# A fused cross-covariance attention and GELU feed-forward kernel: 137 sevenfold sets for 125, one sum of the second product held in PSUM, squares and scalings moved between two engines, and a new order

## The chip, the core and the metric

The kernel runs on one core of one Trainium2 chip. A core has TensorE (PE in the profile; its weight loads are shown apart as PEld), VectorE (DVE), ScalarE (ACT), GpSimd (POOL) and SyncE (SP). Each takes its instructions strictly in the order in which the program gives them, and waits where one of them needs something that is not there yet. SP, POOL and ACT also issue DMA transfers. The metric is the device time of one execution in microseconds (us). Before the change it is 689.86 us, the median of three runs from 689.82 to 689.93.

## What is computed

The reference, cut to what matters:

```python
B, N, C = 4, 6080, 256                   # q, k, v: (B, N, C); w_in: (256, 2048); w_out: (2048, 256)
qn = q / (norm(q, axis=1) + 1e-6)        # norms over the 6080 tokens
kn = k / (norm(k, axis=1) + 1e-6)
s = kn.transpose(0, 2, 1) @ qn / tau     # 256 x 256 for each batch
a = softmax(s)
x = (v @ a).reshape(24320, 256)
h = x @ w_in                             # 24320 x 2048
out = gelu_tanh(h) @ w_out               # 24320 x 256
```

## The kernel before

**Folding.** The kernel never forms x. For each of the four batches it computes `AW = a @ w_in` (256 x 2048, bf16), so that the first product is `v @ AW` and the second `gelu(v @ AW) @ w_out`. The tokens are cut into 25 blocks (`SB`): 23 of 1024 or 960 tokens and two last ones of 512 and 448. A block is two halves of `hc` tokens (512, 480, 256 or 224), and each half is the free side of a matmul.

**First product of a block.** The 2048 features are 16 chunks `fc` of 128, in eight pairs `p`. A pair takes one of two ways. The direct way, `mm1_one` (step `j`, L550 to L558), is two matmuls for one chunk and one half, followed by one Gelu on ACT (`gelu_one`, step `J`, L561 to L570); a pair has four of these, eight matmuls in all. The other way is a *set* (`small` L601, `set_step` L624): seven matmuls `m1` to `m7` on sums of the weights (`sums_w`, DVE) and of the tokens (`sums_v`, DVE) give the same four results, a Strassen-like scheme. In return a set has two more copies on ACT (`cq`, L636, from the sum `rb` into a second PSUM bank `qa`; `y5`, L639, from the bank `qb` into SBUF) and two additions on DVE (`ap`, L641; `ax`, L644). It ends with four Gelus (`G0` L646, `G1` L649, `Gr` L652, `Gx` L655), as the direct way does. Where `cq` puts a copy under a running sum, matmuls on zeros first mark those parts of the bank that no matmul wrote at full width before (L630 to L635).

**Second product of a block.** It is the same scheme at a larger size: DVE forms sums of Gelu results (`sums_g`, steps `T1` to `T4`, each in halves a and b), then come seven products `M1` to `M7` of eight matmuls each, in halves A and B (`product`, L720). They go to three PSUM sums: `u` takes M1, M6, M7 and M4, `p` takes M5 and M3, `c` takes M2 alone (`BANK`, L718). After M1, `x1` copies `u` into SBUF on ACT (`keep`, L737 to L742). After M2, `a11` adds that copy to `c` on DVE (`add_out`, L744 to L748) and `c11` transposes the sum into the output tile (`turn`, L750). `ap`, `ax`, `c12`, `c21` and `c22` do the like for the other quarters. `O0` and `O1` store the rows.

**The next batch's weights.** While a batch is worked on, q and k of the next are loaded (`lq`, `lk`, from POOL's queue), multiplied (`r`: one gram row is two matmuls of 256 columns, L292), squared on ACT (`zq`, `zk`, `square_later`, L253 to L264) and folded on DVE (`f`, L272 to L284). A chain of small steps then gives the exponentials `eT`; `aw` multiplies them with w_in (L498), and `ac` scales the result out of PSUM, for batches 1 to 3 on ACT where the part is in `AW_ACT` (L509) and else on DVE (L511). `lv` casts v through DRAM (POOL's queue, L305), and `lt` loads it transposed (SP's queue, L317).

**The start.** Batch 0 has a path of its own: gram and squares as its rows arrive, then the loads of v, w_in (`win_bf`) and w_out (`wst`, two of 1 MB) on POOL's queue, `scores`, and `first_aw` (L364 to L394), which gives the first 512 of the 2048 columns of `AW`; then the Gelu table is loaded on ACT (L876).

**Order and banks.** After that, the whole program is one list written out by hand, `ORDER`, of 3958 steps such as `12:s5m3` (block 12, set 5, matmul m3), `b2:zq4` or `7:M1A`. Each engine gets its instructions in the order of that list. The eight PSUM banks (`a` to `h`) are handed out in the order in which they were given back (`take`, `give`), so a step that takes a bank waits for the last reader of the bank that came free longest ago.

Of the kernel before, what the change touches and what calls it, by code (L numbers as in the profile page):

```python
# [18 lines left out]
def kernel(  # L19
# [10 lines left out]
    nc = tc.nc  # L30
# [222 lines left out]
    def square_later(b, c, which):  # L253
        n = chunk(c)[1]
        if (b, c) not in SQ:
            SQ[b, c] = sqp.tile([128, CH, 512], BF16, tag="sq", name=f"sq{b}_{c}")
            if n < CH:
                nc.vector.memset(SQ[b, c][REM:, n, :], 0.0)
        t = qk_tiles[b, c, which]
        parts = [(128, slice(0, n))]  # L260
        if n < CH:
            parts.append((REM, slice(n, n + 1)))
        for np_, r in parts:
            nc.scalar.activation(SQ[b, c][:np_, r, which * 256 : which * 256 + 256], t[:np_, r, :], AF.Square)  # L264
# [99 lines left out]
    def first_aw():  # L364
# [21 lines left out]
        for f in range(2):  # L386
            for ic in range(2):
                o = AW[b][:, ic, f * 256 : f * 256 + 256]
                if (f, ic) == (0, 1):
                    nc.scalar.activation(o, ps[f][ic], AF.Copy, scale=rs[:, ic : ic + 1])  # L390
                else:
                    nc.vector.tensor_scalar_mul(o, ps[f][ic], rs[:, ic : ic + 1])
# [178 lines left out]


# [51 lines left out]
    def set_step(m, p, what):  # L624
# [3 lines left out]
        if what == "cq":  # L628
            Q0[m, p], tag = take(("q0", m, p), 1, [128, 512], f"qa{m}_{p}", width=None)
            while WIDTH.get(tag, 0) < hc:  # L630
                w = WIDTH.get(tag, 0)
                e = min(hc, w + 256)
                nc.tensor.matmul(Q0[m, p][:, w:e], lhsT=ones_bf, rhs=zeros_bf[:, 0 : e - w],
                                 start=w == 0, stop=True, skip_group_check=True)
                WIDTH[tag] = e  # L635
# [84 lines left out]
    def product(m, i, half):  # L720
        hc = SB[m][2]
        acc = BANK[i]
        first = (m, acc) not in STARTED
# [11 lines left out]
    XS, CS, OT = {}, {}, {}  # L735

# [33 lines left out]
    def mm2_step(m, what):  # L770
# [3 lines left out]
        elif what == "x1":  # L774
            keep(m, "u", "x1")
# [8 lines left out]
        elif what == "a11":  # L784
            add_out(m, "c", "x1", 0, 0)
            give(("c", m))
# [3 lines left out]
        else:  # L790
            ci, tj = {"c22": (1, 1), "c11": (0, 0), "c12": (0, 1), "c21": (1, 0)}[what]
            if (m, ci, tj) in CS:
                turn(m, ci, tj, CS.pop((m, ci, tj)))
            else:
                acc = {"c12": "p", "c21": "u"}[what]
                turn(m, ci, tj, ACCS[m, acc])
                give((acc, m))

    with tc.manual_schedule():
# [64 lines left out]
        for f0, f1 in ((0, 256), (256, 512), (512, 1024), (1024, 1536), (1536, 2048)):  # L864
            nc.gpsimd.dma_start(out=win_bf[:, :, f0:f1], in_=wi[:, :, f0:f1])
        load_wout(0)
        load_v0(0, 1)
# [6 lines left out]
        pe_vt_copy(0, 0, 1)  # L874
        first_aw()
        nc.scalar.preload_act_table(AF.Gelu_apprx_tanh)  # L876
# [7 lines left out]
        def step(b, what):  # L884
# [9 lines left out]
            elif what[:2] in ("zq", "zk"):  # L894
                square_later(b, int(what[2:]), "qk".index(what[1]))
# [66 lines left out]
1:j31 1:J41 0:J41 0:s7Gx 1:vs1 1:j20 b1:r0.1 1:J21 0:M5A b1:r0.2 1:J31 b1:zq0 b1:r0.3 b0:w03 b1:zk0
0:T2a b1:lk3 1:s3m5 0:M1B b1:r1.0 0:T3b b1:r1.1 1:J20 0:x1 2:lt0 0:T1b b1:lq3 b1:r1.2 1:j11 :pS2
0:T2b 0:M5B b1:zq1 0:M6A 0:y5 1:s3cq 3:lt1 0:M6B 0:ap 1:J11 b1:f0.1 1:s3m6 b1:r1.3 0:T4a b1:lq4
1:s3y5 1:vs2 1:J51 1:s3ap 1:s3m2 1:s4m5 1:s3G0 b1:zk1 0:M7A 1:s4m1 0:M3A 1:s4y5 0:M7B 1:s4cq b1:r2.0
b1:f1.1 b1:zq2 3:lt0 1:s3m7 1:s4m6 0:ax 1:s4m2 b1:r2.1 1:s4ap 1:s3ax b1:zk2 1:s4G0 b1:r2.2 0:T4b
1:s3m3 b1:lk4 0:M3B 1:s4m3 1:s5m1 1:s4m7 b1:f1.2 b1:zk3 0:M4A 1:s4G1 1:s3G1 1:s3Gx 0:c12 1:s3m4
1:s5cq 1:s5m5 1:s4ax 0:M4B 1:s3Gr b1:f2.1 1:s5m2 1:s4Gx b1:r2.3 1:s5y5 b1:lk5 1:s5m6 1:s4m4 0:c21
1:s5G0 b1:r3.0 1:s5ap 1:s4Gr 1:s6m1 1:s6m5 0:M2A 1:s5m7 b1:lq6 b1:zq3 b1:f1.3 1:s6y5 1:s5ax 1:s5m3
b1:r3.1 b1:r3.2 0:M2B b1:r3.3 0:c22 1:s6cq 4:lv1 1:s5G1 1:s6m6 1:s7m1 1:s5Gx 1:s7cq 0:a11 1:s5m4  # L970
1:s6m2 1:s6ap 1:T3a 1:s5Gr b1:lq5 b1:r4.0 b1:r4.1 1:s7m5 1:s6m7 1:s7m6 1:s6G0 1:s6m3 1:s7m2 1:s7y5
1:s6ax 4:lv0 1:s7ap b1:r4.2 2:j20 1:s6G1 2:j51 2:s3m1 1:s6m4 b1:r4.3 1:s7m3 1:s7G0 1:s6Gx 1:s7m7
1:M1A 2:J20 2:j00 1:s7G1 b1:f3.1 b1:f3.2 b1:f3.3 1:s6Gr 2:s3cq 1:s7ax 2:J51 1:T1a 2:j10 1:s7m4
1:s7Gx 1:M1B 2:J00 2:vs0 2:s3m2 1:s7Gr 2:j41 2:s3G0 2:j01 2:j11 2:J10 1:T3b 2:j30 2:J01 1:M5A 2:s3m5
2:J30 b1:r5.0 1:T1b 2:j31 2:vs1 2:J11 2:J41 2:j40 2:vs2 2:s3m6 2:s3y5 1:x1 1:T2a 2:J31 2:s3ap 2:s4m1
b1:lk6 1:T2b 1:M5B 2:J40 1:y5 2:s3m7 1:M6A 2:s3m3 2:s4m5 1:M6B b1:r5.1 2:s3ax 2:s4cq 2:s3m4 b1:zk4
2:s4m6 2:s3G1 2:s4y5 2:j21 2:s4m2 1:T4a 2:s3Gx 2:s3Gr 1:ap 2:J21 1:M7A 2:s4ap 2:s4m7 1:T4b 2:s5m5
b1:lk7 2:s4m3 2:s5m1 1:M3A b1:zk5 1:M3B 2:s4G1 1:M7B b1:r5.2 2:s5y5 b1:zq5 2:s5cq b1:zq4 b1:f3.4
2:s4ax 2:s4m4 2:s5m2 0:c11 1:c12 b1:r5.3 6:lv0 2:s4G0 b1:lk8 0:O1 2:s5m6 1:ax 1:M4A 2:s5ap 2:s5G0
4:lt1 2:s6m1 b1:lq7 b1:f5.1 2:s4Gx 2:s5m3 2:s6cq 2:s6m5 2:s5G1 1:c22 2:s5m7 2:s6y5 1:M4B 2:s4Gr  # L980
2:s5ax b1:lq8 2:s5Gx 1:c21 2:s6m2 2:j50 2:s5m4 2:s6G0 2:T3a b1:zq6 2:s6m6 b1:r6.0 2:s7m5 2:s6ap
1:M2A 2:s7m1 2:s5Gr 2:J50 1:M2B 2:s6m3 2:s6m7 2:s7cq b1:f4.1 1:O1 b1:r6.1 3:j50 1:a11 b1:r6.2 3:j10
2:s7y5 2:s6G1 3:J50 2:s6ax 2:s7m6 1:c11 3:j31 b1:r6.3 0:O0 3:J10 2:s7m2 2:s6Gx 2:s7ap 2:T1a 2:M1A
2:s7m7 2:s7G0 2:s6m4 2:s7m3 3:j01 2:s7ax b1:zk6 b1:r7.0 3:J31 b1:zk7 b1:r7.1 b1:r7.2 2:s7Gx b1:r7.3
2:T2a 2:M1B 3:j21 2:s7G1 2:s6Gr 2:s7m4 b1:f5.2 3:j30 3:J01 2:s7Gr 3:j51 b1:f6.1 2:T3b 3:J21 3:j00
3:j20 2:x1 3:J00 2:M5A 3:s3m1 3:J51 3:J20 2:T1b 3:vs0 2:T2b 3:s3cq b1:lq9 3:vs1 2:M5B b1:f5.3 3:j40
3:s3m5 3:J30 2:y5 3:s3y5 2:M6A 3:J40 3:s3m2 3:s3G0 3:s4m1 3:s4cq b1:zq7 2:T4a 3:s3m6 b1:r8.0 2:M6B
3:s3ap 3:vs2 b1:lq10 2:ap 3:s3m3 3:s4m5 3:s4y5 3:s3m7 3:s4m6 3:s3ax 3:s4m2 b1:lk9 1:O0 3:s4G0 3:s3Gx
3:s4ap 2:M7A 2:M3A b1:zk8 3:s4m7 3:s3m4 3:s3G1 3:s3Gr 3:j11 2:M7B 3:s4ax 3:J11 3:j41 3:s4Gx 3:s5m5
2:T4b b1:r8.1 2:M3B b1:f5.4 3:s4m4 b1:lk10 2:ax 3:s5m1 3:J41 b1:zq8 b1:f7.1 3:s4m3 2:c12 2:M4A  # L990
3:s5cq b1:r8.2 3:s4Gr 3:s5m2 3:s5m6 b1:f7.2 2:c22 3:s5y5 3:s5ap 3:s6m1 2:M4B 3:s4G1 3:s5G0 3:s6m5
b1:f7.3 3:s6cq 3:s5m7 b1:f7.4 b1:zq9 2:M2A 3:s6y5 3:s6m6 b1:r8.3 b1:r9.0 3:s6m2 2:M2B 2:c21 b1:zk9
4:lt0 3:s5ax 3:s5m3 6:lv1 3:s6ap 3:s6G0 3:s6m7 3:s7m1 3:s5Gx b1:f8.1 4:j10 2:a11 3:s5G1 3:s6m3
b1:lk11 3:s5m4 3:s7cq b1:r9.1 3:s7m5 b1:r9.2 4:J10 b1:r9.3 3:s6ax 3:s7y5 3:s6G1 b1:lq11 3:s6m4
3:s7m2 3:s7m6 b1:r10.0 4:j11 3:T3a 3:s6Gx 3:s6Gr b1:f9.1 3:s7ap 4:J11 3:M1A 3:s7m7 3:s5Gr 3:T1a
3:s7m3 4:j00 3:M1B 4:s3m1 3:s7G1 4:j50 3:s7ax 3:T2a 3:s7m4 4:J00 b1:f9.2 4:j40 3:s7Gx 3:x1 b1:r10.1
3:T3b 7:lv1 4:vs0 4:J50 4:s3cq 4:J40 3:T1b 3:M6A 3:s7Gr 4:j30 3:s7G0 4:vs1 4:s3m2 4:j41 4:s3m5
# [280 lines left out]
```

## Time and profile before

| | before |
|---|---|
| median of 3 runs | 689.86 us |
| the profiled execution | 689.49 us, of which the span from first to last instruction is 687.7 us |
| granted TensorE clock | 0.998 of full speed |
| TensorE busy | 667.5 us in 3483 matmuls |
| VectorE busy | 623.9 us in 916 instructions |
| ScalarE busy | 632.8 us in 1205 instructions |
| first direct matmul of block 0 | 37.58 us after the start of the span |
| first matmul of the second product | 62.88 us |
| 16 DMA engines | 78.80 MB, 115 GB/s mean |

An instruction's duration in the profile is not its price where an engine has the next one ready: a matmul of 512 columns is recorded with 0.379 us and the next begins 0.216 us after it; Gelus of 512 columns, recorded with 0.66 to 0.69 us, follow each other every 0.49 us. The prices below are such distances from start to start. The rows of the engines therefore add up to more than the engine's busy time.

### The profile page before, as it was taken

The numbers are of one execution on the slowest core, as the hardware profiler recorded it, in microseconds if no ns is written. First come the engines' busy times: TensorE is split into PE (matmuls) and PEld (weight loads), VectorE is DVE, ScalarE is ACT, GpSimd is POOL, SyncE is SP. The second block draws the span as 40 slices with busy tenths as digits, with TensorE's granted clock in tenths as the row PEclk, the third lists the DMA queues.
The fourth block names the chain that finished last, engine by engine and source line by source line (L and its number), as shares of the span: only waits on it lengthen the run. The fifth ranks groups of instructions, "written<-read, shape, count | busy, mean of one in ns | idle before, by whom it ended". The sixth has DMA issues, their size and how long they took to land.

```text
span 687.7 us, 10235 instructions
## 1 busy us (share of the span) xinstructions
PE 667.5 (97%) x3483; PEld 334.9 (49%) x3483; DVE 623.9 (91%) x916; ACT 632.8 (92%) x1205; POOL 89.1 (13%) x163
## 2 busy tenths in 40 slices
PE   3989999999999999999999999999999999999997
PEld 2844445454445455444444545445444444444455
DVE  3589898999998899999999998999999999999995
ACT  5389999999999999999989999999989999999963
POOL 4331211121000212020001102111000000000001
PEclk9999999999999999999999999999999999999999
DMA  9999677649564899854454789850828524433416
GB/s 241 208 264 167 100 120 132 113 81 157 94 99 86 140 180 153 151 86 77 91 99 73 130 145 162 153 90 17 131 38 157 95 51 86 73 58 61 74 34 118
DMA packets 165093, 78.80 MB, mean 115 GB/s; under 512 B 148992, under 2 KB 153472, under 8 KB 164320
## 3 DMA queue, kind: packets, MB, share of 16 engines
q0 software_dynamic: 18000, 39.72, 34.8%
q1 hardware_dynamic: 145792, 37.14, 29.5%
q10 hardware_dynamic: 1248, 1.28, 0.6%
q8 instruction: 27, 0.44, 0.3%
q14 instruction: 26, 0.21, 0.1%
HBM read 78.91 MB, written 36.57 MB: 168 GB/s over the span
## 4 chain that ended last, share of the span: by engine, by line
PE 88%; DMA 7%; ACT 4%; issue 0%; DVE 0%; POOL 0%; ACTq 0%; POOLq 0%
PE u L732 23%; PE j L557 15%; PE rb L616 15%; PE p L732 11%; PE qb L616 7%; PE c L732 6%; PE G L292 4%; DMA qk<-in_k_dram 4%; PE qa L616 4%; PE awp L498 2%; DMA k<-in_k_dram 1%; ACT g L569 1%; DMA win_bf<-in_moe_w_in_dram 1%; ACT sq L264 1%; ACT g L649 0%
## 5 line engine op out<-in xcount | busy, mean ns | idle before, releaser
L732 PEld LDWEIGHTS <-wcomb 128*128 128x128 bf16 x1400 | 136.8, 98 | 142.8 <-issue 1.1
L569 ACT ACTIVATE g<-j 128x512 bf16<-128x512 f32 (+1 forms) x252 | 154.1, 672 | 4.0 <-PE j L557 3.2
L557 PE MATMUL j<-vT,aw 128*128 128x512 bf16 (+2 forms) x552 | 147.8, 376 | 1.1 <-ACT g L569 0.5
L732 PE MATMUL u<-t,wcomb 128*128 128x512 bf16 (+3 forms) x600 | 145.6, 368 | 0.0
L732 PE MATMUL p<-g,wcomb 128*128 128x512 bf16 (+3 forms) x400 | 97.2, 368 | 0.0
L641 DVE TENSOR_TENSOR qb<-rb,yw 128x512 f32<-128x512 f32 (+2 forms) x125 | 84.3, 679 | 8.4 <-ACT yw L639 3.3
L616 PE MATMUL rb<-tv,sw 128*128 128x512 bf16 (+2 forms) x250 | 91.0, 374 | 0.0
L644 DVE TENSOR_TENSOR xw<-rb,yw 128x512 f32<-128x512 f32 (+2 forms) x125 | 83.1, 669 | 6.3 <-PE rb L616 4.1
L636 ACT ACTIVATE qa<-rb 128x512 f32<-128x512 f32 (+2 forms) x125 | 80.1, 643 | 5.6 <-PE rb L616 4.1
L655 ACT ACTIVATE g<-xw 128x512 bf16<-128x512 f32 (+2 forms) x125 | 83.8, 674 | 1.1 <-DVE xw L644 1.0
L649 ACT ACTIVATE g<-qb 128x512 bf16<-128x512 f32 (+2 forms) x125 | 79.5, 642 | 5.5 <-PE qb L616 5.3
L557 PEld LDWEIGHTS <-aw 128*128 128x128 bf16 x552 | 53.8, 98 | 59.8 <-issue 3.8
L639 ACT ACTIVATE yw<-qb 128x512 f32<-128x512 f32 (+2 forms) x125 | 78.7, 638 | 2.0 <-PE qb L616 1.8
L646 ACT ACTIVATE g<-qa 128x512 bf16<-128x512 f32 (+2 forms) x125 | 79.4, 643 | 1.1 <-PE qa L616 0.9
L652 ACT ACTIVATE g<-rb 128x512 bf16<-128x512 f32 (+2 forms) x125 | 79.7, 644 | 0.2
L616 PEld LDWEIGHTS <-sw 128*128 128x128 bf16 x500 | 48.9, 98 | 52.4 <-issue 1.1
L713 DVE TENSOR_TENSOR t<-g,g 128x2048 bf16<-128x2048 bf16 (+3 forms) x50 | 57.9, 1158 | 3.5 <-ACT g L566 2.2
L305 POOL DMA_DIRECT2D vb<-in_v_dram x47 | 24.2, 515 | 270.4 <-PE rb L616 164.1
L705 DVE TENSOR_TENSOR g<-g 128x2048 bf16<-128x2048 bf16 (+3 forms) x50 | 58.1, 1163 | 0.4
L711 DVE TENSOR_TENSOR t<-g,g 128x2048 bf16<-128x2048 bf16 (+3 forms) x50 | 58.1, 1164 | 0.3
L715 DVE TENSOR_TENSOR t<-t,g 128x2048 bf16<-128x2048 bf16 (+3 forms) x50 | 57.5, 1159 | 0.1
L616 PEld LDWEIGHTS <-aw 128*128 128x128 bf16 x375 | 36.7, 98 | 37.8
(131 smaller groups left out, 1005.5 us busy)
## 6 DMA issues: line engine op xcount, KB each, us to landing
out_dram<-ot SPq DMA_DIRECT2D x160, 128.0 KB, 3.2
vb<-in_v_dram POOLq DMA_DIRECT2D x37, 256.0 KB, 4.7
k<-in_k_dram POOLq DMA_DIRECT2D x33, 256.0 KB, 4.7
q<-in_q_dram POOLq DMA_DIRECT2D x33, 256.0 KB, 5.4
out_dram<-ot SPq DMA_DIRECT2D x24, 120.0 KB, 4.8
wst<-in_moe_w_out_dram POOLq DMA_DIRECT2D x2, 1024.0 KB, 11.0
qk<-in_q_dram POOLq DMA_DIRECT2D x3, 512.0 KB, 14.5
qk<-in_k_dram POOLq DMA_DIRECT2D x3, 512.0 KB, 17.1
```

The source lines that it names most:

```text
L557: GATE[0] = nc.tensor.matmul(hp[:, :n].rearrange("p (t x) -> p t x", t=2) if t == 2 else hp[:, :n], lhsT=AW[b][:, cc, fc * 128 : fc * 128 ...
L569: nc.scalar.activation(g[:, t, fc % 8, :hc], hp[:, :hc], AF.Gelu_apprx_tanh)
L616: GATE[0] = nc.tensor.matmul(acc[:, :hc], lhsT=lhs, rhs=rhs, start=i in (1, 5), stop=True, skip_group_check=True)
L636: nc.scalar.activation(Q0[m, p][:, :hc], RB[m, p][:, :hc], AF.Copy)
L639: nc.scalar.activation(YW[m, p][:, :hc], Q1[m, p][:, :hc], AF.Copy)
L641: nc.vector.tensor_add(Q1[m, p][:, :hc], RB[m, p][:, :hc], YW[m, p][:, :hc])
L644: nc.vector.tensor_add(XW[m, p][:, :hc], RB[m, p][:, :hc], YW.pop((m, p))[:, :hc])
L646: nc.scalar.activation(g[:, 0, e, :hc], Q0.pop((m, p))[:, :hc], AF.Gelu_apprx_tanh)
L649: nc.scalar.activation(g[:, 1, e, :hc], Q1.pop((m, p))[:, :hc], AF.Gelu_apprx_tanh)
L652: nc.scalar.activation(g[:, 0, e + 1, :hc], RB.pop((m, p))[:, :hc], AF.Gelu_apprx_tanh)
L655: nc.scalar.activation(g[:, 1, e + 1, :hc], XW.pop((m, p))[:, :hc], AF.Gelu_apprx_tanh)
L732: GATE[0] = nc.tensor.matmul(ACCS[m, acc][:, :hc], lhsT=wcomb[:, w, fc, :], rhs=x[:, fc, :], start=first and k_ == 0, stop=k_ == 3, skip_g ...
```

## The change

Six parts of the text change, and the order.

- `square_later` takes a flag. `zq` and `zk` square on ACT as before; the new step `dk` squares the same piece of k with a multiplication on DVE. In the new order the even pieces of k (18 of 36) are `dk`.
- `AW_ACT` holds all eight parts: the scalings `ac` of batches 1 to 3 are all on ACT. There are 24 of these; 12 were on DVE.
- `first_aw` scales its first 256 columns on DVE in four pieces of 128 and its last 256 on ACT in two. Before it was three pieces of 256 on DVE and one on ACT.
- The Gelu table is loaded ahead of `first_aw` in place of behind it.
- The second piece of v for block 0 is loaded ahead of the first part of w_out.
- `x1` becomes `split_off`: the copy of `u` goes on ACT into a PSUM bank `c` of its own, M2 adds to it there, `a11` is gone and `c11` transposes straight from that bank. The marking of a bank becomes a helper, `flagged`.
- The list: 4017 steps. Counted by kind, what differs is this.

| steps | before | after |
|---|---|---|
| `j` and `J` (direct chunk and its Gelu; 2 matmuls, 1 ACT) | 252 each | 204 each |
| `m1` to `m7`, `cq`, `y5`, `ap`, `ax`, four Gelus (sets) | 125 each | 137 each |
| `a11` | 25 | 0 |
| `zk`, `dk` | 36, 0 | 18, 18 |

The new sets are number 2 of blocks 2 to 4 and 7 to 18 (15 sets, in blocks 11 and 17 with 480 columns). Block 0 loses set 5, and blocks 20 and 22 lose set 1 (three sets of 512 columns). All other steps are as many as before and stand in another order.

```diff
-    def square_later(b, c, which):
+    def square_later(b, c, which, on_act):
...
-            nc.scalar.activation(SQ[b, c][:np_, r, which * 256 : which * 256 + 256], t[:np_, r, :], AF.Square)
+            o = SQ[b, c][:np_, r, which * 256 : which * 256 + 256]
+            if on_act:
+                nc.scalar.activation(o, t[:np_, r, :], AF.Square)
+            else:
+                nc.vector.tensor_mul(o, t[:np_, r, :], t[:np_, r, :])
...
-        for f in range(2):
+        for u in range(2):
             for ic in range(2):
...
+                nc.vector.tensor_scalar_mul(AW[b][:, ic, u * 128 : u * 128 + 128],
+                                            ps[0][ic][:, u * 128 : u * 128 + 128], rs[:, ic : ic + 1])
+        for ic in range(2):
+            nc.scalar.activation(AW[b][:, ic, 256:512], ps[1][ic], AF.Copy, scale=rs[:, ic : ic + 1])
...
+    def flagged(t, tag, hc):
+
+        while WIDTH.get(tag, 0) < hc:
+            w = WIDTH.get(tag, 0)
+            e = min(hc, w + 256)
+            nc.tensor.matmul(t[:, w:e], lhsT=ones_bf, rhs=zeros_bf[:, 0 : e - w],
+                             start=w == 0, stop=True, skip_group_check=True)
+            WIDTH[tag] = e
...
-        first = (m, acc) not in STARTED
+        first = acc != "c" and (m, acc) not in STARTED
...
+    def split_off(m):
+
+        hc = SB[m][2]
+        ACCS[m, "c"], tag = take(("c", m), 1, [128, HALF], f"c{m}", width=None)
+        flagged(ACCS[m, "c"], tag, hc)
+        nc.scalar.activation(ACCS[m, "c"][:, :hc], ACCS[m, "u"][:, :hc], AF.Copy)
...
         elif what == "x1":
-            keep(m, "u", "x1")
+            split_off(m)
...
-        elif what == "a11":
-            add_out(m, "c", "x1", 0, 0)
-            give(("c", m))
...
-                acc = {"c12": "p", "c21": "u"}[what]
+                acc = {"c11": "c", "c12": "p", "c21": "u"}[what]
...
+        load_v0(0, 1)
         load_wout(0)
-        load_v0(0, 1)
         load_v0(1, 0)
...
+        nc.scalar.preload_act_table(AF.Gelu_apprx_tanh)
         first_aw()
-        nc.scalar.preload_act_table(AF.Gelu_apprx_tanh)
...
-AW_ACT = (1, 3, 5, 7)
+AW_ACT = (0, 1, 2, 3, 4, 5, 6, 7)
 ORDER = """
...
-0:j00 b0:aw2 2:lv1 b0:aw3 b0:aw4 b0:ac2 0:j10 b0:aw5 b0:ac4 1:lv1 0:J00 0:j30 0:s5m1 0:J10 0:J30
...
+0:j00 b0:aw3 b0:aw2 0:j30 b0:ac3 0:j10 b1:lq0 b0:ac2 b0:aw5 3:lv0 0:j20 0:J30 b1:lk0 1:lv1 0:J20
...
```

Two stretches of the lists that the prediction refers to, around `x1` of block 20. Before: `20:M1B 20:s7Gx 19:a11 20:s7m4 20:s7m3 20:T2a 21:s2cq 21:j01 21:vs0 20:s7G1 21:j00 20:T3b 21:s2m2 20:M5A 20:s7Gr 21:vs1 21:s1m5 21:J01 21:j11 20:x1 20:M6A`. After: `20:M1B 19:M4B 20:s6G1 21:vs0 20:s7G1 20:s7Gr 21:s1m1 21:s2m1 21:J00 21:J10 21:s1m5 23:lv1 20:T1a 21:vs1 20:x1 21:J01 19:c21 21:s1cq 21:s2cq 20:M2A`.

## The prediction, made before the changed kernel was run

> **What bounds the kernel now.** I read the page's shares first, then the busy time by stretches, then the chain that ended last, and last what TensorE itself waited for.
>
> ```profile
> PE 667.5 (97%) x3483; PEld 334.9 (49%) x3483; DVE 623.9 (91%) x916; ACT 632.8 (92%) x1205; POOL 89.1 (13%) x163
> ...
> PE 88%; DMA 7%; ACT 4%; issue 0%; DVE 0%; POOL 0%; ACTq 0%; POOLq 0%
> ```
>
> Three engines are over 90% busy, so shares alone decide nothing. The chain is 88% TensorE. The stretches (busy us of each engine; the last numbers are clock, DMA share and GB/s) show where it is not:
>
> ```profile
> 37.60:62.90 25.30, 22.00 (x108) 9.63 (x109) 21.94 (x37) 22.89 (x43) 6.56 (x11) 1.00 1.16 240
> 62.90:100.00 37.10, 36.98 (x190) 18.45 (x190) 34.13 (x47) 37.10 (x68) 5.29 (x10) 1.00 0.73 116
> 100.00:650.00 550.00, 550.00 (x2712) 264.43 (x2711) 520.96 (x750) 535.02 (x1026) 58.21 (x107) 1.00 0.62 104
> ```
>
> From 100 to 650 us TensorE has no gap while ScalarE is busy 97% and VectorE 95%: a removed matmul is worth its full distance there, and the two others have 15 and 29 us to spare. Distances from start to start, in the chain and on ScalarE's time line:
>
> ```profile
> 80.14 0.86 PE u L732 x4
> ...
> 103.60 1.73 PE p L732 x8
> ```
>
> ```profile
> 219.94 0.58 ACT L639 ACTIVATE yw<-qb 128x512 f32<-128x512 f32 x1
> 220.42 0.60 ACT L649 ACTIVATE g<-qb 128x512 bf16<-128x512 f32 x1
> 220.89 0.64 ACT L655 ACTIVATE g<-xw 128x512 bf16<-128x512 f32 x1
> 221.41 0.60 ACT L646 ACTIVATE g<-qa 128x512 bf16<-128x512 f32 x1
> 221.89 0.61 ACT L636 ACTIVATE qa<-rb 128x512 f32<-128x512 f32 x1
> 222.41 0.61 ACT L652 ACTIVATE g<-rb 128x512 bf16<-128x512 f32 x1
> ```
>
> Eight matmuls in 1.73 us are 0.216 us each. On ScalarE `y5` costs 0.48 us, `G1` 0.47, `Gx` 0.52, `G0` 0.48, `cq` 0.52, and by the same reading `Gr` 0.47, a direct Gelu 0.49, a square 0.94 and a scaling `ac` 0.48. On VectorE a 512-wide `ap`, `ax`, `a11` or transpose costs 0.60, a fold of 128x1024 in bf16 0.59 and an `ac` 0.66.
>
> **More sets: -2.6 us.** A set has seven matmuls where the direct way has eight. Twelve more net: 13 - 3 at 512 columns and 2 at 480, so 10 x 0.216 + 2 x 0.203 = 2.6 us of TensorE. Following the banks through the takes and gives of both lists, no `flagged` matmul is issued in either, as none shows in the rows of before.
>
> **ScalarE and VectorE.** ScalarE: 24 copies more, 12 x (0.52 + 0.48) = +12.0; Gelus are equal in number, -0.2; 18 squares leave, -16.9; 12 scalings come, +5.8; `x1` into PSUM at `cq`'s price, 25 x 0.04 = +1.0; one more scaling in `first_aw`, +0.5. Sum +2.2 us. VectorE: 24 additions, +14.4; 25 `a11` leave, -15.0; 18 squares come at the fold's price (same tile, same type, also two SBUF inputs), +10.6; 12 scalings leave, -7.9. Sum +2.1 us. Both lie beside TensorE, which covers them with 15 and 29 us in the long stretch; uncovered they would cost 2 us each. That is the total. Along the lists, the most by which ScalarE's listed work runs ahead of TensorE's in any stretch is 4.0 us after and 6.6 before; for VectorE 4.6 after against 4.9 before, except at the start.
>
> **The start: -2.45 us.** The first matmul of the second product starts at 62.88 us, 25.30 us after the first direct one. The list asks TensorE for 20.4 us until there (89 matmuls of 512 columns, 16 transposes, a gram row), so 4.9 us are lost. Two named waits:
>
> ```profile
> PE vt_ps L333 <- DMA v<-in_v_dram: 0.9, 1, 0.9
> PE awp L498 <- DMA win_bf<-in_moe_w_in_dram: 0.4, 1, 0.4
> ```
>
> and then ScalarE, which in the chain of that stretch runs without a break:
>
> ```profile
> 53.82 0.65 ACT g L569
> 54.46 0.49 ACT g L649
> 54.95 0.98 ACT g L569 x2
> 55.93 0.51 ACT g L655
> ```
>
> The second piece of v was issued at 34.37 behind 1 MB of w_out and read at 44.37; it goes ahead of that megabyte, so the 0.9 goes, and w_out is issued 0.8 later. Its first reader was at 43.19 and comes after 6.4 us of VectorE's list, about 45; if it is late, VectorE's weight sums for set 7 stand behind it. The third w_in part, which landed at 39.40, is asked for two direct chunks later, so the 0.4 goes. ScalarE's list up to M1A falls from 22.2 us of work (over TensorE's 20.4) to 14.5 (under 17.0), since two preparations of w_out on ScalarE move behind it, one set leaves and fewer Gelus precede. What is late next is VectorE: 15.7 us up to M1A, but then 8.9 us of it within 5.0 us of TensorE (three sums of w_out, four sums of Gelus, two of tokens), 3.9 us behind at worst; the first matmul that needs what follows, set 3's m3 of block 1, stands 5 us of TensorE later. So I take half of the 4.9 us, 2.45, between 0 and 4.9; a loss below zero would need VectorE's burst to be longer than that 5 us.
> The Trainium skill (Trainium Kernel Development and Optimization, section Performance Expectations) calls matmul busy time a bad measure, because matmuls are pipelined. By the busy row only 25.30 - 22.00 = 3.3 us are lost, half is 1.65, and the forecast would be 0.8 later; the trace agrees with the page, as a matmul recorded with 0.38 us is followed after 0.216.
>
> Table load: it takes 1.28 us, at 37.51 now; in its new place it fills 36.28 to 36.92, where ScalarE waits for the reciprocal, and ends at 37.56. Two scalings of 0.47 then end at 38.5; the first Gelu needs a chunk that stands behind two `aw` products and is ready at 39.3. So 0, and at most 0.6 without that cover. The four 128-wide scalings on VectorE delay the first direct matmul by some 0.1 us (estimate: 0.27 each, from 0.40 at 256 and 0.66 at 512).
>
> **`x1` into PSUM: +1.5 us.** This adds a wait. Before, M2 went to a fresh bank and only M6 waited for `x1`; now M2 waits for it, and everything on TensorE queues behind M2. I summed for each block TensorE's work between M1's end and the first matmul that waits, and ScalarE's up to and with `x1`. Block 20: 14 matmuls, 3.0 us, against 2.9 before; 7 matmuls, 1.5 us, against 2.9 (three set Gelus, two direct ones, the copy) after. The shortage, block by block, hangs on how far ScalarE is along the list when M1 ends:
>
> | ScalarE against TensorE at M1's end | before: shortage, blocks | after |
> |---|---|---|
> | 1 us ahead | 0, none | 1.3 us, 3 |
> | 0.5 us ahead | 0.4 us, 1 | 3.3 us, 6 |
> | level | 2.3 us, 5 | 7.8 us, 12 |
> | 0.5 us behind | 6.5 us, 12 | 15.4 us, 19 |
>
> All that the matmuls lose behind 62.88 us is 682.59 - 62.88 - (637.5 - 20.4) = 2.6 us, so ScalarE is not behind; it is level or ahead. I take 1.5 us, near the row of 1 us ahead, as no wait of TensorE is named after 63 us; ends 0 and 7.8. The bank of `c` is held for 5.4 us of TensorE's list on the mean, 2.9 before, but the median distance from a bank's release to its next use grows from 0.86 to 1.02 us: nothing for that.
>
> **Loads.** POOL's issues cost 0.52 to 0.54 us beside VectorE's additions, which have two SBUF inputs. Only two took 0.91 and 0.85, at 55.62 and 60.06, both beside a cast on VectorE. The squares are of the first kind. TensorE waits for no transfer after 63 us, and the least distance from a transposing load to its first use grows from 0.9 to 4.1 us. So 0; if each of 18 squares held up one issue by 0.4 us, that cover would still hide it.
> The Trainium skill (SBUF — State Buffer, section Who interferes with whom) speaks against the change here: a VectorE instruction with two SBUF inputs contends with a GpSimd instruction that reads SBUF, and a cast can block it entirely. The trace agrees on the cast and shows no delay from two inputs; by the page 18 issues could come late, at most the 0.4 above.
>
> **Tail.** VectorE ends the kernel with seven instructions back to back from 680.38 to 683.05; one goes (`a11`), and the last transpose still follows the last matmul. 0.
>
> **Sum.** 689.49 (the profiled execution; its span is 687.7, and 1.8 lie around it) - 2.6 - 2.45 + 1.5 = 685.95. The median of the runs is 0.37 above the profiled execution, so 686.3.
>
> **Rivals.** (1) *The start is healed and `x1` costs nothing*: 689.86 - 2.6 - 4.9 = 682.4. For it: the lighter ScalarE list; against: VectorE's burst. (2) *The start's loss only changes its engine*: 689.86 - 2.6 + 1.5 = 688.8, no change that can be told. For it: 8.9 us of VectorE in 5.0. (3) *Slower: M2 waits for `x1`*, in half of the blocks: with ScalarE level, 689.86 - 2.6 - 2.45 + 7.8 = 692.6. It decides from a price of 5 us on, ScalarE less than 0.25 us ahead. For it: ScalarE's load in the long stretch rises to (535 + 2) / (550 - 2.6), 98% of TensorE's; against: the 2.6 us. (4) *The change does not do what it says*: banks turn out unmarked and 25 x 2 matmuls of 256 columns (0.108 us) come in, 686.3 + 5.4 = 691.7; the count of banks speaks against it.
>
> **Chances.** Forecast 0.58 (own range 684.3 to 688.4), rival 1 0.14, rival 2 0.11, rival 3 0.15, rival 4 0.02. A measurement of this kernel can tell about 0.2% (1.4 us) from no change. Faster by more is forecast and rival 1, 0.72; within it rival 2, 0.11; slower rivals 3 and 4, 0.17. The range 682.3 to 691.3 leaves out the far part of rivals 3 and 4 and a little below rival 1.
>
> **What would show it.** TensorE's matmuls: 12 fewer. First matmul of the second product at 57 us (37.6 + 17.0 + half of the 4.9) if the start is as I say; no wait for v or w_in named; VectorE without a gap from there to 66 us. `c` matmuls waiting for the copy in at most a few blocks: if TensorE has named waits on it of several us in total, the +1.5 is wrong and rival 3 is at work. If TensorE's busy row shows gaps in the long stretch with another releaser, the new order is what I have misread.

## The result and the profile after

The changed kernel takes 694.89 us (median of 4 runs, 694.18 to 695.25), the kernel before 689.84 beside it: ratio 1.0072, with an interval of 1.0055 to 1.009. It is slower by 5 us, where 686.3 was forecast, and lies outside the range of 682.3 to 691.3.

The first two lines are the page of the changed kernel: busy time, then the chain that ended last.

```profile
PE 667.2 (96%) x3471; PEld 334.2 (48%) x3471; DVE 626.0 (90%) x922; ACT 635.8 (92%) x1224; POOL 87.7 (13%) x163
...
PE 82%; DMA 8%; ACT 6%; issue 2%; DVE 1%; POOL 1%; SPq 0%; POOLq 0%; DVEq 0%; ACTq 0%
```

Twelve matmuls fewer, as forecast, ScalarE 3.0 us busier and VectorE 2.1. Against the page of before, TensorE's share of the chain has fallen from 88% to 82%, which such shares alone do not explain. The stretches (busy us of PE, PEld, DVE, ACT and POOL, then clock, DMA share, GB/s) show where:

```profile
40.00:55.00 15.00, 14.82 (x84) 7.29 (x83) 13.89 (x27) 14.26 (x30) 5.76 (x11) 1.00 1.12 278
55.00:58.00 3.00, 1.11 (x7) 0.39 (x4) 1.75 (x3) 2.72 (x5) 0.00 (x0) 1.00 0.96 181
58.00:64.30 6.30, 0.00 (x0) 0.00 (x0) 0.00 (x0) 0.00 (x0) 0.00 (x0) 0.74 1.18 164
64.30:68.00 3.70, 3.68 (x11) 1.48 (x12) 2.19 (x4) 1.08 (x2) 0.00 (x0) 0.52 0.09 19
```

Up to 55 us the changed kernel is ahead: TensorE is busy 14.8 of the 15 us, where the kernel before has this:

```profile
40.00:55.00 15.00, 12.74 (x69) 5.77 (x67) 12.92 (x23) 13.20 (x25) 3.20 (x6) 1.00 1.15 252
```

Then every engine stands still for 6.3 us while the DMA engines are full, and TensorE goes on at half the clock: 11 matmuls in 3.7 us. Its own time line names what it waited for, and the chain of that stretch names what stood behind that:

```profile
54.87 1.03 PE L739 MATMUL u<-g,wcomb 128*128 128x512 bf16 x4
55.73 0.38 PE L296 MATMUL G<-k,q 128*128 128x256 bf16 x2
64.32 1.03 PE L560 MATMUL j<-vT,aw 128*128 128x512 bf16 x2 [8.21 <-DMA vT<-vb]
```

```profile
41.77 11.62 DMA vb<-in_v_dram
53.38 0.02 issue
53.40 10.87 DMA vT<-vb
```

The matmul is `1:j41`, the first to read the second half of block 1's tokens. That half is cast into DRAM by `1:lv1` (11.62 us from issue to landing) and then loaded transposed by `1:lt1` (10.87 us). In the kernel before, this load was issued at 50.87 and took 6.9 us, and `1:j01` was the first to read the half, 1.2 us after the landing:

```profile
vT<-vb SPq DMA_TRANSPOSE x1, 6.9
```

```profile
58.96 0.59 PE L557 MATMUL j<-vT,aw 128*128 128x512 bf16 x2
```

So the 8.2 us are 2.9 of an earlier use (56.1 in place of 58.96) and 6.5 of a later landing (64.3 in place of 57.8), less those 1.2.

The 5.76 us between the two profiled executions can be laid out with the prediction's own lists. First direct matmul: 37.48 against 37.58, -0.1. From there to the first matmul of the second product 0.4 us are lost (54.87 - 37.48 - 17.0) where it was 4.9: -4.5. Sets: -2.6. Behind that point TensorE loses 15.5 us (its last matmul ends at 688.32; 688.32 - 54.87 - 617.9 of list) where it lost 2.6: +12.9, of which 8.2 is the one wait and 1.7 the half clock behind it (run 4); most of the rest is still there without the wait (run 5). Tail and what lies around the span: +0.1.

### The profile page after: what moved, and what is told of

The parts are those of the page before. It is cut to its first block, busy times and chain, and to the rows that moved or that the text cites. A ratio compares the mean times of both kernels' runs of the same rounds, so it can differ in the third digit from the quotient of the medians.

```text
span 693.4 us, 10265 instructions
## 1 busy us (share of the span) xinstructions
PE 667.2 (96%) x3471; PEld 334.2 (48%) x3471; DVE 626.0 (90%) x922; ACT 635.8 (92%) x1224; POOL 87.7 (13%) x163
## 4 chain that ended last, share of the span: by engine, by line
PE 82%; DMA 8%; ACT 6%; issue 2%; DVE 1%; POOL 1%; SPq 0%; POOLq 0%; DVEq 0%; ACTq 0%
PE u L739 21%; PE rb L628 15%; PE j L560 12%; PE p L739 10%; PE qb L628 8%; PE c L739 5%; PE G L296 4%; PE qa L628 4%; DMA vT<-vb 3%; DMA vb<-in_v_dram 2%; PE G L199 1%; DMA q<-in_q_dram 1%; DMA st<-in_q_dram 1%; ACT aw L512 1%; ACT g L572 1%
## 5 line engine op out<-in xcount | busy, mean ns | idle before, releaser
L560 PE MATMUL j<-vT,aw 128*128 128x512 bf16 (+2 forms) x456 | 126.8, 379 | 9.3 <-DMA vT<-vb 8.7
L572 ACT ACTIVATE g<-j 128x512 bf16<-128x512 f32 (+1 forms) x204 | 122.0, 656 | 12.6 <-PE j L560 12.4
L648 DVE TENSOR_TENSOR qb<-rb,yw 128x512 f32<-128x512 f32 (+2 forms) x137 | 92.6, 679 | 7.4 <-PE rb L628 3.3
L628 PE MATMUL rb<-tv,sw 128*128 128x512 bf16 (+2 forms) x274 | 99.2, 374 | 0.0
L651 DVE TENSOR_TENSOR xw<-rb,yw 128x512 f32<-128x512 f32 (+2 forms) x137 | 91.4, 669 | 7.7 <-PE rb L628 6.0
L662 ACT ACTIVATE g<-xw 128x512 bf16<-128x512 f32 (+2 forms) x137 | 91.9, 674 | 0.5 <-DVE xw L651 0.5
L643 ACT ACTIVATE qa<-rb 128x512 f32<-128x512 f32 (+2 forms) x137 | 86.8, 637 | 3.0 <-DVE ot L768 1.4
L646 ACT ACTIVATE yw<-qb 128x512 f32<-128x512 f32 (+2 forms) x137 | 86.2, 635 | 2.3 <-PE qb L628 2.1
L653 ACT ACTIVATE g<-qa 128x512 bf16<-128x512 f32 (+2 forms) x137 | 86.8, 636 | 0.9 <-PE qa L628 0.8
L659 ACT ACTIVATE g<-rb 128x512 bf16<-128x512 f32 (+2 forms) x137 | 86.0, 637 | 0.6 <-PE rb L628 0.5
L628 PEld LDWEIGHTS <-sw 128*128 128x128 bf16 x548 | 53.7, 98 | 56.4 <-issue 1.6
L560 PEld LDWEIGHTS <-aw 128*128 128x128 bf16 x456 | 44.7, 99 | 54.6 <-DMA vT<-vb 9.4
```

Of the source, the lines that this page charges most:

```text
L560: GATE[0] = nc.tensor.matmul(hp[:, :n].rearrange("p (t x) -> p t x", t=2) if t == 2 else hp[:, :n], lhsT=AW[b][:, cc, fc * 128 : fc * 128 ...
L572: nc.scalar.activation(g[:, t, fc % 8, :hc], hp[:, :hc], AF.Gelu_apprx_tanh)
L628: GATE[0] = nc.tensor.matmul(acc[:, :hc], lhsT=lhs, rhs=rhs, start=i in (1, 5), stop=True, skip_group_check=True)
L643: nc.scalar.activation(Q0[m, p][:, :hc], RB[m, p][:, :hc], AF.Copy)
L646: nc.scalar.activation(YW[m, p][:, :hc], Q1[m, p][:, :hc], AF.Copy)
L648: nc.vector.tensor_add(Q1[m, p][:, :hc], RB[m, p][:, :hc], YW[m, p][:, :hc])
```

## The experiments

All were run beside the kernel before, which took 689.5 to 689.7 us in each group; the ratios are to that. The theory after the result: the loss is that one wait. Two causes were open: A, the cast stands too late in POOL's queue; B, the crowd: too many other loads are under way in this stretch. C in the expectations is the prediction's rival 3, M2's wait for the copy `x1`. Other readings were that the half clock behind the wait is a loss of its own, and that the change would be no faster without the wait.

**1. The cast earlier.** Theory A alone.

```diff
-0:j00 b0:aw3
+0:j00 1:lv1 b0:aw3
...
-b1:lk0 1:lv1 0:J20
+b1:lk0 0:J20
```

> The changed kernel with one load moved: the cast of block 1's second half of v is issued first on POOL's queue behind the first direct chunk, ahead of q0, block 3's v and k0 (it stood behind them). Theory A (place in the queue): the half came late because three loads stood ahead of it; moved, it is issued about 3 us earlier, the wait of 8.2 us and the cold clock behind it go, and the time is 683 to 685. Theory B (crowd): the half and its transposing load are slow because ten loads of 256 KB are in flight with them; moving one changes the issue by 3 us only, of which the wait keeps about 5 us, and the time is 689 to 692. Theory C (the wait on x1 of the forecast's rival 3): no change, 694 to 695.

Measured: 695.13 us, ratio 1.0082 (1.0064 to 1.0101). The cast was issued 3.5 us earlier, at 38.24, and landed 3.8 us earlier, at 49.6. The transposing load then took 14.5 us and landed at 64.1, as in the changed kernel. A falls: an earlier place brings nothing. B's 689 to 692 is missed too, since not even the 3.5 us came through. The time is near C's, but not for its cause: the same 8.2 us are named, for `vT`.

**2. Loads later.** Theory B alone.

```diff
-1:j41 :pA12
+1:j41 3:lv1 b1:lk2 b1:lq2 4:lv0 :pA12
```

(The four leave their places ahead of `1:j41`.)

> The changed kernel with four loads moved back: v of block 3 (second half) and of block 4 (first half) and the third pieces of q and k of batch 1 are issued only behind the first direct chunk of block 1 that needs the late half (they stood 10 to 3 us ahead of it). The late half keeps its place in the queue, behind three loads. Theory A (place): the half lands as late as before, 692 to 695. Theory B (crowd): its transposing load shrinks from 10.9 us to the 6 to 7 us of the kernel before, the wait falls to 3 us or less, and the time is 685 to 689. Theory C: 694 to 695.

Measured: 691.05 us, ratio 1.0021 (1.0012 to 1.0031). The transposing load shrank from 10.9 to 4.8 us with nothing done to it. TensorE's waits:

```profile
PE G L296 <- DMA q<-in_q_dram: 3.0, 1, 3.0
...
PE j L560 <- DMA vT<-vb: 2.1, 1, 2.1
```

B's wait of 3 us or less holds, its 685 to 689 us doesn't: the four were badly chosen, and the third piece of q, now issued at 60.31, is late itself. (The profiled execution, 692.71, is among the slower of ten from 689.53 to 693.03.)

**3. Both.** Cast first, and `3:lv0` postponed besides.

> The changed kernel with both edits, and block 3's first half of v moved back as well. Theories A and B: no named wait on the transposing load is left, TensorE goes through the start at full clock, and the time is 682 to 685, which is what the forecast's own terms give without this wait (2.6 us of matmuls and 3 to 4.9 us of the start). Theory C: 694 to 695.

Measured: 693.17 us, ratio 1.0052 (1.0033 to 1.007); the expected time was missed. The transposing load was issued 3.5 us earlier than in run 2 and took 8.7 us in place of 4.8, so it landed no earlier, at 58.7, and the gram rows waited for q as in run 2 (2.5 us). The place of the cast brought nothing a second time.

**4. The clock.** 76 matmuls of zeros, 256 columns wide, into `1:j41`'s own bank keep TensorE at work during the wait.

```diff
+        if (m, fc, t) == (1, 4, 1):
+            for i in range(76):
+                nc.tensor.matmul(hp[:, 0:256], lhsT=ones_bf, rhs=zeros_bf, start=True, stop=True)
```

> The changed kernel with 76 matmuls on zeros (256 columns each, 8.2 us) put on TensorE ahead of the late chunk, into the bank that this chunk then overwrites: the wait stays, but TensorE has work in it. If the drop of the granted clock behind the wait (0.66 in the profile of 60 to 70 us) costs time of its own, about 2 us (matmuls at 0.43 us in place of 0.216 from 64.3 to 68.2), the time falls to 692 to 693.5. If it costs nothing, because transfers bound that stretch anyway, it stays at 694 to 695.5.

Measured: 694.54 us, ratio 1.0073 (1.0058 to 1.0088). TensorE's time line:

```profile
56.20 8.46 PE L560 MATMUL j<-zeros_bf,ones_bf 128*128 128x256 bf16 x76
64.50 0.60 PE L563 MATMUL j<-vT,aw 128*128 128x512 bf16 x2
...
67.52 1.03 PE L742 MATMUL u<-g,wcomb 128*128 128x512 bf16 x4
```

The clock stays at 1.00, and the steps from `1:j41` to the next matmuls of `u` take 3.0 us; in the changed kernel they began at 64.32 and 69.06 and took 4.7. So the half clock costs 1.7 us at its place. In the kernel's time nothing of it can be told: the median is 0.35 us lower, but the ranges overlap, and the ratio to the kernel before is 1.0073 with the filling and 1.0072 without. The second expectation holds. The wait is the loss, the clock its small companion.

**5. The loads in the order of their use.** The three casts of v for blocks 3 and 4 leave the stretch altogether, `2:lv0` goes behind `1:j41`, `lq1` goes ahead of `lk2` and `lq2`.

```diff
-b0:aw5 3:lv0 0:j20
+b0:aw5 0:j20
...
-0:Ja0 3:lv1 2:lv0 0:s7m1
+0:Ja0 b1:lq1 0:s7m1
...
-0:vs2 b1:lk2 0:j21 1:vc00 b1:lq2 0:s6G0
+0:vs2 0:j21 1:vc00 0:s6G0
...
-0:jb1 4:lv0 0:s7y5
+0:jb1 0:s7y5
...
-1:j30 0:J01
+1:j30 b1:lk2 b1:lq2 0:J01
...
-1:j41 :pA12
+1:j41 2:lv0 :pA12
...
-2:lt1 1:s3Gx
+2:lt1 3:lv0 1:s3Gx
...
-b1:lk5 1:s4m3
+b1:lk5 3:lv1 1:s4m3
...
-b1:lq5 b1:dk4
+b1:lq5 4:lv0 b1:dk4
```

(`2:lt0` moves from behind `b1:r1.0` to ahead of `b1:zq0`.)

> The changed kernel with its early loads put in the order in which their data is used: the two v loads of block 3 and the one of block 4 (first used by TensorE more than 20 us later) leave the stretch ahead of 1:j41 altogether, 2:lv0 goes right behind it, lq1 goes ahead of the third pieces of k and q, and these (lk2, lq2) are issued some 3 us later than before. Crowd theory (the start asks for more transferred bytes before 57 us than arrive, and the loss is set by what is late): three 256 KB loads at about 1.2 us each leave, so the transposing load of v needs under 6 us and the third piece of q is there by 61 us; the waits for vT and q sum to under 3 us, and the time is 685 to 688 us. Rival (the order of the sets and squares would lose the same microseconds to other engines once the transfers are out of the way): the named waits go, but others come in their place, and the time is above 690.

Measured: 685.44 us, ratio 0.9939 (0.9927 to 0.9951), and the same four stretches:

```profile
40.00:55.00 15.00, 14.76 (x82) 7.23 (x82) 13.79 (x27) 14.26 (x30) 3.74 (x7) 1.00 1.10 263
55.00:58.00 3.00, 3.00 (x18) 1.50 (x17) 2.88 (x5) 3.00 (x7) 0.51 (x1) 1.00 0.94 145
58.00:64.30 6.30, 6.24 (x34) 3.23 (x34) 6.30 (x7) 6.30 (x15) 0.50 (x1) 1.00 0.82 139
64.30:68.00 3.70, 3.70 (x19) 1.77 (x19) 3.70 (x6) 3.70 (x8) 1.07 (x2) 1.00 0.50 60
```

No engine stands still and the clock stays. No step of computation was touched, only the places of eight loads, and 9.5 us are gone. So these loads are the whole reason why the changed kernel is slower, and they hid a gain: this version is 4.2 us faster than the kernel before.

**6. The same, with the cast ahead of w_out's second megabyte.** In the preamble; `lk2` and `lq2` were also put 4.1 us earlier (issued at 49.56 and 50.08), behind `0:j81`.

```diff
         load_v0(1, 0)
+        cast_v(1, 1)
         load_wout(1)
```

> As the run before, and in addition the late half of block 1's v is cast into DRAM ahead of the second megabyte of w_out, and lk2 and lq2 are issued at 50 us in place of 52. Crowd theory with a queue served in order: the half of v stood behind that megabyte (it landed at 49.6 and 50.0 us whether issued at 38.2 or 38.6), so it now lands at 45 to 47 us and its transposing load ends before 55 us, ahead of its use: no wait for vT, 684 to 686 us. Rival (transfers of the software queue aren't served in order, or w_out's second part is then late): vT lands no earlier than 49 us, or a wait of VectorE for wst of over 1 us shows, and the time is as in the run before or longer.

Measured: 690.66 us (686.84 to 693.0), ratio 1.0006 (0.9988 to 1.0024): a miss. The cast landed at 47.0 as expected, and still TensorE waited, as the chain shows:

```profile
36.33 10.63 DMA vb<-in_v_dram
46.97 0.02 issue
46.98 13.65 DMA vT<-vb
60.64 0.05 issue
60.69 1.05 PE j L560 x2
```

Data that were there at 47.0 needed 13.65 us for the last hop. A queue served in order explains the cast; it does not explain this. The twelve executions spread over 6 us, those of run 5 over 1.2; the profile shows one near the middle.

**7. The use later.** All loads as in the changed kernel; what reads the late half stands behind `0:M5A`.

```diff
-1:j41 :pA12 0:s7m4
+:pA12 0:s7m4
...
-0:T2b 0:M5A 0:x1
+0:T2b 0:M5A 1:j41 1:J41 1:j31 1:vs0 1:vs1 1:s3m1
...
+1:j01 1:s3ap 1:J51 1:J11 0:x1
```

> The changed kernel with all its loads where they are; the steps that read the late half of block 1's v (1:j41 to 1:J11, the first sums vs0 and vs1, and set 3 as far as it stands there) are put behind the other steps up to 0:M5A, some 5 us of TensorE's list. If the 8.2 us are only a use that comes ahead of its data, the wait for vT shrinks by what TensorE can do in the meantime, 3 to 5 us, and the time is 690 to 692 us. If the work that is put ahead is itself not ready (VectorE's sums T1 to T3 for M1B and M5A, the third piece of q), TensorE waits as long on something else and the time stays at 694 to 696.

Measured: 692.29 us, ratio 1.0047 (1.0031 to 1.0063), 0.3 us above the first expectation. The second holds in part: no wait for v is left, and in its place the gram rows wait 5.5 us for `q1`, which stands behind `lk2` and `lq2` in the same queue. With this crowd another load was late in its place.

**8. Run 6 with `lk2` and `lq2` at 54 us, as in run 5.** Nothing else differs from run 6.

> The version that cast block 1's late half of v ahead of the second megabyte of w_out, with lk2 and lq2 issued at 54 us again as in the spread version; nothing else differs. What is to be told apart is why its transposing load took 13.7 us (46.98 to 60.7) with data that were there at 46.9. Theory 'lands when the software queue has run dry': in seven runs the transposing load landed 0.5 to 2.3 us after the last load that stood in that queue, whenever it was issued; here the last load ahead of the pause (q1, issued at 46.1) lands at about 55.2, so the transposing load lands at 55.7 to 57, over 8 us after its issue, TensorE waits 0 to 0.7 us for it, and the time is that of the spread version, 685 to 686 us. Rival 'the transposing load has a price of its own that grows only with the bytes that flow beside it': it would land by 53 us. If it lands at 60 again, both fall.

Measured: 684.64 us, ratio 0.9928 (0.9916 to 0.9939). The transposing load's line among the DMA issues, and TensorE without a gap:

```profile
vT<-vb SPq DMA_TRANSPOSE x1, 9.0
```

```profile
55.00:58.00 3.00, 3.00 (x19) 1.64 (x18) 3.00 (x6) 3.00 (x7) 0.52 (x1) 1.00 1.12 186
58.00:64.30 6.30, 6.25 (x35) 3.25 (x34) 6.30 (x7) 6.30 (x14) 0.50 (x1) 1.00 0.75 132
```

It was issued at 46.96 and landed at 55.96, inside the expected 55.7 to 57, though its data had lain ready for 9 us: the rival falls. Of runs 5 and 8, which differ by less than their intervals, neither is clearly the faster; both beat both kernels. The nine traces in which loads or their use stand differently, together (times in us from the span's start; casts and loads from POOL's time line and the DMA issues):

| kernel | 256 KB loads issued, 36 to 53.4 us | cast of the half, issue to landing | its transposing load, issue to landing | landing of the last load issued over 5 us before that landing | TensorE's longest wait for it |
|---|---|---|---|---|---|
| before | 7 | 40.8 to 50.9 | 50.9 to 57.8 | 56.0 | 0 |
| after | 11 | 41.8 to 53.4 | 53.4 to 64.3 | 63.5 | 8.2 |
| 1 cast earlier | 11 | 38.2 to 49.5 | 49.6 to 64.1 | 63.6 | 8.2 |
| 2 loads later | 7 | 41.9 to 53.4 | 53.5 to 58.3 | 57.4 | 2.1 |
| 3 both | 6 | 38.6 to 50.0 | 50.0 to 58.7 | 56.5 | 2.5 |
| 5 in order of use | 5 | 41.8 to 52.0 | 52.0 to 56.2 | 54.5 | 0 |
| 6 cast ahead of w_out | 7 | 36.3 to 46.9 | 47.0 to 60.7 | 61.4 | 4.3 |
| 7 use later | 11 | 41.7 to 53.4 | 53.4 to 64.2 | 63.4 | 0 |
| 8 as 6, two loads later | 5 | 36.3 to 47.0 | 47.0 to 56.0 | 55.2 | 0 |

The fifth column is the end of the backlog of the software queue, the one of POOL's loads (younger loads, in before, 5 and 8, are left out; the limit of 5 us was chosen with the traces at hand). The issue of the transposing load varies by 6 us, and its landing doesn't follow it: it comes between 0.7 us ahead of the end of the backlog (run 6, against the 0.5 us behind it that the expectation names as the least) and 2.3 us behind it.

The packets in the DMA engines show how. A transposing load is 1056 packets of some 250 bytes; the packets of POOL's loads (`q0`) have some 2 KB. While both queues have work, they move packet for packet, as in run 1 from 54 to 60 us:

```profile
q0 software_dynamic: 435, 1.03, 90.8%
q1 hardware_dynamic: 435, 0.11, 14.2%
```

At this rate, 73 packets in a microsecond, 1056 would need 14.5 us (an estimate). It ends sooner where `q0` runs dry: in run 8 the two queues move 192 and 190 packets from 51 to 53 us, and then `q1` moves 438 from 53 to 54 beside 62 of `q0`. So each load in the other queue holds the small packets up, and an earlier issue brings them only turns beside that queue.

**9 and 12. `x1` into SBUF again,** on the version of run 5, to price that part alone: first with the addition `a11` right behind M2, then directly ahead of `c11`. Block 24 keeps the new way.

```diff
-        first = acc != "c" and (m, acc) not in STARTED
+        first = (m, acc) not in STARTED and (m, acc) not in ACCS
...
-            split_off(m)
+            split_off(m) if m == 24 else keep(m, "u", "x1")
...
+        elif what == "a11":
+            add_out(m, "c", "x1", 0, 0)
+            give(("c", m))
```

> The spread version with the copy x1 into SBUF again for blocks 0 to 23, c's bank taken at M2 and the addition a11 (VectorE) right behind M2; block 24 keeps the new way. It prices that part of the change alone: 24 additions of 0.60 us come back on VectorE (14.4 us of its list), ScalarE's 24 copies are 0.04 us cheaper, M2 waits for no copy. Theory of the prediction (M2's wait for the copy costs TensorE 1.5 us, VectorE's additions lie beside TensorE): 683 to 684.5 us. Rival (the additions pay: without them VectorE has 14 us more room and its users come earlier): slower than the spread version, 687 us or more. No difference over 0.7 us: the part costs and brings nothing.

Measured: 710.4 us, ratio 1.0306 (1.029 to 1.0321). This is on the rival's side and far beyond it. VectorE's waits suggest that a good part is the place I gave the additions, where its whole queue stood behind M2's matmuls:

```profile
DVE c L761 <- PE c L739: 17.2, 16, 3.6
```

> As the run with x1 in SBUF and a11 right behind M2, which took 710.4 us and in which VectorE stood 17.2 us waiting for M2's matmuls at that addition: here a11 stands directly ahead of c11, where the order has VectorE come to this sum anyway. If the 25 us came from the place of the additions, VectorE no longer waits there and the time comes back to 683 to 690 us; at or below 684 the wait of M2 for the copy is worth its 1.5 us, near 690 the 14.4 us of additions are. If they came from the changed rotation of the PSUM banks (c's bank is taken at M2 in place of x1, so all later takes shift), or from VectorE's room altogether, the time stays above 698 and the price of this part alone can't be read in this order.

Measured: 695.59 us, ratio 1.0084 (1.007 to 1.0097). That wait is gone and 14.8 us with it; 10.2 us over run 5 remain. The chain has 16% of VectorE where run 5 has 1%:

```profile
PE 64%; DVE 16%; ACT 7%; DMA 6%; issue 4%; SPq 1%; POOL 0%; DVEq 0%; POOLq 0%; ACTq 0%
```

The time falls between the expected cases. VectorE is 13.9 us busier than in run 5 (639.5 against 625.6), and its share of the chain says that a part of this is not covered in this order. But taking `c`'s bank at another step also shifts every later bank, and that was not separated, so neither the additions nor M2's wait for the copy have a price of their own from these runs.

**10. Squares and scalings as before the change,** on run 5.

```diff
-b1:dk0
+b1:zk0
...
-AW_ACT = (0, 1, 2, 3, 4, 5, 6, 7)
+AW_ACT = (1, 3, 5, 7)
```

(All 18 `dk` become `zk`.)

> The spread version with all 36 squares of k on ScalarE and half of the scalings ac on VectorE, as before the change: ScalarE's list grows by 18 x 0.94 - 12 x 0.48 = 11.2 us (to 96% of TensorE's list over the whole), VectorE's shrinks by 18 x 0.59 - 12 x 0.66 = 2.7. The prediction put the move at nothing either way, as work beside TensorE. By that: 685 to 686 us. Rival (ScalarE is so full that the 11 us come onto the path in part, through the banks that it frees): 687 to 692 us.

Measured: 706.02 us, ratio 1.0238 (1.0224 to 1.0251), far beyond either expectation. The chain:

```profile
PE 51%; ACT 35%; DVE 6%; DMA 4%; issue 3%; POOL 0%; DVEq 0%; ACTq 0%; POOLq 0%
```

ScalarE is 10.9 us busier than in run 5 (646.0 against 635.1) and becomes the bound in a third of the chain; besides, its copies wait 4.3 us (`cq`) and 1.6 us (`x1`) for scalings that now stand in VectorE's queue. How the 20.6 us divide between squares and scalings was not tried.

**11. The start as before the change,** on run 5: order of the loads of v and w_out, place of the table load, pieces of `first_aw`.

```diff
-        load_v0(0, 1)
         load_wout(0)
+        load_v0(0, 1)
...
-        nc.scalar.preload_act_table(AF.Gelu_apprx_tanh)
         first_aw()
+        nc.scalar.preload_act_table(AF.Gelu_apprx_tanh)
```

> The spread version with the three edits of the start undone: the second piece of v for block 0 behind the first megabyte of w_out, the Gelu table loaded behind first_aw, and first_aw scaled in four pieces of 256 (three on VectorE). By the prediction's terms the 0.9 us wait of the transposes for that piece of v comes back, or part of it, as it would land some 3 us later (44.4 in place of 41.5) and is read at about 45: 685 to 686.5 us, the first direct matmul within 0.2 us of where it is. If the order of those two loads is what healed the start, the first matmul of the second product moves from 55 towards 57 us and the time to 687 or more.

Measured: 687.78 us (686.7 to 689.78), ratio 0.9975 (0.9965 to 0.9985): 2.3 us slower than run 5, as the second expectation has it. In the profiled execution, the slowest of ten, the first matmul of the second product starts at 59.27 in place of 55.16. The piece of v lands at 44.6 in place of 41.5, and TensorE waits longer for it than before the change (0.9 us), since the new order comes to it at 42.4 in place of 43.5:

```profile
PE vt_ps L337 <- DMA v<-in_v_dram: 2.3, 1, 2.3
```

Behind this wait too the clock falls to half (0.50 from 45 to 47 us). What the faster executions waited for no profile shows.

## Why the prediction was wrong, point by point

**Loads, the step that failed.** "TensorE waits for no transfer after 63 us, and the least distance from a transposing load to its first use grows from 0.9 to 4.1 us. So 0". That 0 is the term that failed: it measured 8.2 us of waiting and, with the loads moved, 9.5 us of the kernel's time. The distance was measured in TensorE's list from the place of the step `lt`. What counts is when the data land, and that was 10.9 us behind the issue, and the issue itself waited for a cast that had taken 11.6. And "no transfer after 63 us" was read where the DMA share is 0.62 to 0.73, while the use in question lies ahead of that, in a stretch where the share is over 1: by the list at 58.96 us before, 1.2 us behind the landing, and at 56 us after. I had looked at POOL's issues for their cost on POOL (0.5 us each, which stayed right) and not for what they put into the queue: eleven loads of 256 KB from 36 to 53.4 us where before had seven. With the loads put in the order of use the step's 0 nearly comes true (0.6 us for a later half of v is left), and so does the forecast: 685.4 for 686.3. That this is so close is in part luck, as two errors offset each other: the start gave 2.4 us more than forecast, `x1` and the order behind it cost 1.1 more.

**Sets, -2.6: right in the count.** Twelve matmuls fewer, no marking matmuls; the microseconds were not measured apart.

**Start, -2.45: right in kind, too small.** The loss fell by 4.5 us in the changed kernel and by 4.8 in run 5 (first second-product matmul at 55.16, 17.1 us behind the first direct one at 38.03). VectorE's burst, for which I took only half, delayed nothing that a wait names. "What is late next is VectorE" was wrong: late next was v. Undoing the edits of the preamble costs 2.3 us in run 5's order (run 11); what they would bring in the order of before was not tried.

**`x1`, +1.5.** Run 5 bounds it together with all else behind the first second-product matmul: TensorE loses 678.23 - 55.16 - 617.9 = 5.2 us there where before lost 2.6. So +2.6 for `x1` and the rest of the order together. No wait of M2 for the copy is named in either trace, as the forecast said it would show at most in a few blocks. Its share stays open (runs 9 and 12).

**ScalarE and VectorE, 0: nothing speaks against it for the change as a whole, but it was wrong as a way of thinking.** With the wait gone, the two stand at 635.1 and 625.6 us busy (+2.3 and +1.7, for +2.2 and +2.1 in the sum) and the time is near the forecast. But I wrote that uncovered they would cost 2 us each, as if each move had spare time of its own beside it. Undone alone, the squares and scalings cost 20.6 us; the additions, with the shifted banks, 10.2. My reading is that the parts cover each other, as the list is written for this division of work; no list was written anew for another division.

**Table load and tail, 0: right.** The load stands from 36.33 to 37.61 us in ScalarE's wait; the end of the span lies 5.1 us behind the last matmul in both kernels.

**Sum for run 5:** first matmul +0.45, start -4.8, sets -2.6, `x1` and order +2.6: -4.35; the profiled executions differ by -4.36. The last term is what the others leave, so that the sum closes proves nothing. Rival 1 (start healed) had the start right, rival 3 the sign of the changed kernel, for another reason. That a transfer becomes the wait was none of the four.

## What to carry to other kernels

When a new order uses data earlier, follow each load from its issue through its queue to its landing, every hop of it, and count what else the same stretch puts into the DMA engines; a distance in instructions is not enough there. Count packets as well as bytes: here a load of many small packets took turns, one for one, with a queue of large ones. If a transfer is late, move away the loads that aren't needed yet before moving the late one forward: here the first was worth 9.5 us and the second nothing that can be told. In a list written by hand, judge the parts of a change together: what one of them costs when it is undone alone belongs to that list.

## What the runs showed of the hardware

- Loads in the software queue land in the order of their issue, 1.2 us apart for 256 KB while it is full and the transposing load hasn't begun (49.7, 50.9, 52.1, 53.4 and 54.6 in the changed kernel), so the flight grew from 3.5 us for a load alone in the queue (issued at 71.25) to 9.5 to 12.3 in a full one.
- A transposing load on SP's queue, 3.7 to 4.7 us in the median of a kernel's 47, took 8.7 to 14.5 us beside a full software queue. The Trainium skill (DMA: Bandwidth & Descriptors, section Queues, rings and completion order) says that each DMA engine takes turns between its queues, packet by packet. The trace agrees: 435 packets of each queue in run 1 from 54 to 60 us, and in the changed kernel 243 and 236 from 57.4 to 60.4. In runs 6 and 8, alike up to 49.5 us, the load was issued at 47.0; from 50 to 56 us its 1056 packets all moved in run 8 and 565 in run 6, where two more loads stood in the other queue.
- None of its packets moved in the first 3 us in runs 6 and 8 (from 47.0 to 50) and in the changed kernel (from 53.4 to 56.4). What it waits for there stays open.
- After 8.2 us of waiting TensorE ran at a clock of 0.52 for 3.7 us, matmuls of 512 columns 0.43 us apart in place of 0.216. The Trainium skill (TensorE: Matmul & The Clock Gate, section What's actually happening) gives half the clock until about 3.4 us of work have passed; the trace agrees. Shorter waits were enough too: the clock fell to 0.50 behind 2.3 us in run 11, 2.5 in run 3 and 3.0 in run 2, and stayed at 1.00 behind 2.1 us in run 2. Of the 1.7 us lost at the place nothing can be told in the kernel's time (run 4).
